# The tail of a Winograd convolution: inner rows transposed ahead of the last silu, the last 32 rows gathered by GpSimd

## The chip, the cores and the metric

The kernel runs on one core of a Trainium2 chip. The metric is the device time of one execution in microseconds (us). Three runs of the kernel before took 187.9, 187.98 and 188.08 us, so its median is 187.98. One execution more was profiled: it took 187.82 us, and the profile covers a span of 186.0 us of it.

## What is computed

A convolution of width 3 along the sequence, a batch norm with given mean and variance, and silu:

```python
xp = jnp.pad(x, ((0, 0), (1, 1), (0, 0)))          # x: 2 x 2048 x 1024, bf16
y = sum(jnp.einsum('bsc,cd->bsd', xp[:, k:k + S, :], w[k]) for k in range(3))
inv_std = 1.0 / jnp.sqrt(var + 1e-5)
y = (y - mean) * (g * inv_std) + b
return silu(y)                                     # 2 x 2048 x 1024, bf16
```

## The kernel before

**Tiling.** The convolution is done by Winograd's method: R = 6 rows of the output are made from 8 products (NJ = 8) instead of 18. The 2048 rows of one batch are NB = 342 blocks of 6 rows (the last block holds 2). TensorE first multiplies windows of x by a constant matrix (L322), and ScalarE or VectorE takes the result to `T_sb`: channels on the partitions, and for each of 8 positions one column per block. The weights of a tile of 128 output channels are turned into three pairs of sums and differences (`u0`, `u1`, `u2`), most of it by GpSimd (L188).

**Units.** A unit is one tile `dc` of 128 output channels and one batch `bi`, 16 in all, in the order of `dc` and then `bi`. A unit makes 8 products of 8 matmuls each (`product`, L368) into four of the eight PSUM banks, and neighbours alternate between banks 0 to 3 and 4 to 7. VectorE combines the products (L386), and ScalarE applies scale, bias and silu (`silu`, L391) and writes `yT`: 128 channels on the partitions, then 6 rows of a block, then 384 places for the blocks. Rows 1 to 4 of a block (inner) are ready when product 6 of the unit is combined. Row 0 and row 5 (outer) need one more product each, made with the raw weights `wch`.

**Stores.** For all but the last two units the DMA turns `yT` (`turn`, L554) into `o`, blocks on the partitions, and SP's queue stores `o` (`store`). For the last two units `put` (L515) turns the rows on TensorE against an identity (L525, one 128x128 transpose per row and group of 128 blocks), one copy brings them from PSUM to `o` (L526), and DMAs store them (L531). Blocks 336 to 341 (the last 32 rows of the batch) do not fit the DMA's shape and go out by `put_rest`: two small DMAs on GpSimd's queue, 30 rows (L542) and 2 rows (L546).

**The last unit** is cut in two halves: `h0`, the larger, holds blocks 128 to 341 in banks 4 to 7, and `h1` blocks 0 to 127 in banks 0 to 3. The order of the work is written out by hand (the program keeps the order of each engine as written). After the products 1 to 6 of h1 have been issued, the kernel before goes on so, L668 to L674:

- `h0.put(inner)`: 8 transposes into bank 5, one copy of 128x1024, two stores on SP's queue (128 and 80 blocks).
- `h1.silu_inner()`: two silus.
- `h1.both(...)`, L409: h1's product 0 into bank 0, then h0's outer rows (4 transposes into bank 6, a copy of 128x512, two stores on SP's queue), then product 7 into bank 3, then one silu that reads banks 0 and 3 as one strided operand and writes rows 0 and 5 of `yT`.
- `h1.put(inner)`: 4 transposes into bank 1, a copy of 128x512, a store on ScalarE's queue (ACTq).
- `h0.put_rest`: the two DMAs on GpSimd's queue.
- `h1.put(outer)`: 2 transposes into bank 2, a copy of 128x256, a store on ScalarE's queue.

Each DMA of SP's and ScalarE's queue counts on one of eight semaphores, in turn, and waits for the DMA eight before it. At the end of the program SP waits for these eight one after the other, in the order of their numbers, and then for the other engines.

`load_w` (L132) brings one of the three taps of the weights for a pair of tiles `dc` (L139), or for one of the two if `half` is given. The third pair after the first, tiles 6 and 7, is loaded behind unit 8 (L645).

Of the kernel before, what the change touches and what calls it, by code (L numbers as in the profile page):

```python
# [8 lines left out]
ACT = mybir.ActivationFunctionType  # L9
ALU = mybir.AluOpType  # L10
FP32 = mybir.dt.float32
BF16 = mybir.dt.bfloat16
# [3 lines left out]
P = 128  # L16
R = 6
# [9 lines left out]
def kernel(  # L27
# [10 lines left out]
    nc = tc.nc  # L38
    B, S, C = x.shape
    D = w.shape[2]  # L40
    CT, DC = C // P, D // P
    NB = -(-S // R)
# [22 lines left out]
    ps = pspool.tile([P, 8, 512], FP32, name="ps")  # L65
    T_sb = [tpool.tile([P, CT, NJ, NB], BF16, name=f"T_sb{bi}") for bi in range(B)]

    rows = consts.tile([4 * DC, P], BF16, name="rows")
# [63 lines left out]
    def load_w(pair, k, half=None):  # L132

        if (pair, "tile") not in raw:
            raw[pair, "tile"] = wpools[pair % 2].tile([P, 3, CT, 2, P], BF16, name=f"wch{pair % 2}")
        wch = raw[pair, "tile"]
        h0, h1 = (0, 2) if half is None else (half, half + 1)
        cols = slice((2 * pair + h0) * P, (2 * pair + h1) * P)
        nc.sync.dma_start(  # L139
            out=wch[:, k, :, h0:h1].rearrange("p c h d -> p c (h d)"), in_=w_all[:, k, :, cols]  # L140
        )
        clock["dma"] += 1400.0 * (h1 - h0)
        for h in range(2):
            raw[2 * pair + h] = wch[:, :, :, h]
# [3 lines left out]
    def idle(work):  # L148
        if work:
            work.pop(0)()  # L150
# [79 lines left out]
    def prepare_second(dc):  # L230


        w0, w2 = raw[dc][:, 0], raw[dc][:, 2]

        def times4(tap):
            t = spool.tile([P, CT, P], BF16, name="w1x2")
            nc.scalar.mul(t, tap, 4.0)
            busy("act", CT * P)
            return t

        def even(q, t, h):
            sums[dc, q] = epool.tile([P, CT, P], FP32, name=f"e{q}")
            nc.gpsimd.tensor_tensor(sums[dc, q], t, h, op=ALU.add)

        def first():
            even_part(dc, 0, nc.gpsimd)
            transform_w(dc, 0)

        def second():
            even(1, times4(w2), w0)  # L250

        def third():
            double_w(dc, nc.scalar)
            transform_w(dc, 1)

        def fourth():
            even(2, times4(w0), w2)
            transform_w(dc, 2)

        return first, second, third, fourth  # L260

    prm = consts.tile([P, 4, DC], BF16, name="prm")
    scale = consts.tile([P, DC], FP32, name="scale")
    beta = consts.tile([P, DC], FP32, name="beta")

    ident = consts.tile([P, P], BF16, name="ident")
# [77 lines left out]
    class Unit:  # L344
# [9 lines left out]
        def __init__(self, dc, bi, b0, lo=0, hi=NB):  # L354
            self.dc, self.bi, self.b0, self.lo, self.hi = dc, bi, b0, lo, hi
            self.bank = [ps[:, b0 + q, lo:hi] for q in range(4)]
            self.low, self.mid, self.high = (ps[:, b0 + q:b0 + q + 2, lo:hi] for q in range(3))
            self.yT = yts[bi]

        def product(self, q, j, add, between):  # L360
            dc = self.dc
            nsl = slice(self.lo, self.hi)
            for ct in range(CT):
                if j == 0 or j == NJ - 1:
                    lhsT = raw[dc][:, 0 if j == 0 else 2, ct]
                else:
                    lhsT = wts[dc, (j - 1) // 2][:, (j - 1) % 2, ct]
                nc.tensor.matmul(  # L368
                    self.bank[q], lhsT=lhsT, rhs=T_sb[self.bi][:, ct, j, nsl],
                    start=not add and ct == 0, stop=ct == CT - 1, skip_group_check=add,  # L370
                )
                clock["pe"] += (self.hi - self.lo) / 2.35
                between()
# [12 lines left out]
            nc.vector.scalar_tensor_tensor(out=out, in0=in0, scalar=scalar, in1=in1, op0=ALU.mult, op1=op1)  # L386
            busy("dve", (self.hi - self.lo) * (2 if len(out.shape) > 2 else 1))

        def silu(self, rows, src):
            dc = self.dc  # L390
            nc.scalar.activation(  # L391
                self.yT[:, rows, self.lo:self.hi], src, ACT.Silu, bias=beta[:, dc:dc + 1], scale=scale[:, dc:dc + 1]
            )

        def silu_inner(self):
            self.silu(slice(2, 4), self.y23)
# [7 lines left out]
        def last(self, between):  # L404

            self.product(3, NJ - 1, True, between)
            self.silu(R - 1, self.bank[3])

        def both(self, between, then):  # L409

            self.product(0, 0, True, between)
            then()
            self.product(3, NJ - 1, True, between)
            self.silu(slice(0, R, R - 1), ps[:, self.b0:self.b0 + 4:3, self.lo:self.hi])

        def run_first(self, between, left, following):

# [97 lines left out]
        def put(self, o, rows, bank, evac, queues, blocks=None):  # L515

            i0, i1 = min(rows), max(rows)
            every = slice(i0, i1 + 1, 1 if i1 == i0 else (i1 - i0) // (len(rows) - 1))
            blocks = blocks or range(self.lo // P, -(-self.hi // P))
            n = min(self.hi - self.lo, P)  # L520
            v = ps[:, bank].bitcast(BF16)[0:n, 0:len(rows) * len(blocks) * P]
            v = v.rearrange("p (i k d) -> p i k d", i=len(rows), k=len(blocks))
            for a, i in enumerate(rows):
                for q, k in enumerate(blocks):
                    nc.tensor.transpose(v[:, a, q], self.yT[:, i, k * P:k * P + n], ident)  # L525
            evac(o[0:n, every, blocks[0]:blocks[-1] + 1], v)  # L526
            outs = out[self.bi, :, self.dc * P:(self.dc + 1) * P]
            full = S // R
            for q, k in zip(queues, blocks):
                hi = min((k + 1) * P, full // 16 * 16)  # L530
                q.dma_start(  # L531
                    out=outs[k * P * R:hi * R].rearrange("(p i) d -> p i d", i=R)[:, every],
                    in_=o[0:hi - k * P, every, k],
                )

        def put_rest(self, o, queue):

            full = S // R
            lo = full // 16 * 16
            k, p0 = lo // P, lo % P  # L540
            rows = out[self.bi, :, self.dc * P:(self.dc + 1) * P]
            queue.dma_start(  # L542
                out=rows[lo * R:full * R].rearrange("(p i) d -> p i d", i=R), in_=o[p0:p0 + full - lo, :, k]
            )
            k, p0 = full // P, full % P
            queue.dma_start(  # L546
                out=rows[full * R:S].rearrange("(p i) d -> p i d", p=1), in_=o[p0:p0 + 1, 0:S % R, k]
            )
# [51 lines left out]
    class Between:  # L600


        n = done = 0
# [20 lines left out]
    between = Between()  # L624
# [3 lines left out]
    for i, (dc, bi) in enumerate(seq[:-1]):  # L628
        unit = Unit(dc, bi, i % 2 * 4)
        if i == 0:  # L630
            unit.run_first(between, left[0], prepare_second(1))
        else:
            unit.run(
                between,
                prev.rest_first(between) if i == 1 else
                prev.rest(between, *((4, 5) if i >= len(seq) - 3 else (5, 4) if i == 2 else (5, 6)))
                + ([(1, lambda: idle(act_work)), (1, lambda: idle(dve_work))] if i == 3 else []),
                2 if i == 2 else dc + 2 if bi == 1 and 0 < dc < DC - 2 else None,
                i == 2,
            )  # L640
        if i == 0:
            xwin_scope.close()
            olast = ctx.enter_context(tc.tile_pool(name="olast", bufs=3))
            wpools[1] = ctx.enter_context(tc.tile_pool(name="wpool1", bufs=1))
        if i in (0, 4, 8):  # L645
            for k in range(3):
                load_w(i // 4 + 1, k)
        if i == len(seq) - 2:
            prev.turn(olast, ((1, R), (0, 1)))
        elif prev:  # L650
            prev.turn()
        if before:
            before.store(late if i == len(seq) - 2 else ())
        before, prev = prev, unit
    before.store(late)
    dc, bi = seq[-1]
    sp, ac = nc.sync, nc.scalar
    inner, outer = tuple(range(1, R - 1)), (0, R - 1)
    to_v, to_s = nc.vector.tensor_copy, nc.scalar.copy
    o = olast.tile([P, R, NK, P], BF16, name="o")  # L660
    h0 = Unit(dc, bi, 4, P, NB)
    h0.run(between, prev.rest(between, 5, 5) + [(5, lambda: prev.put(o, inner, 1, to_v, (sp, sp), (0, 1)))])
    h1 = Unit(dc, bi, 0, 0, P)
# [2 lines left out]
        (3, lambda: prev.put(o, inner, 1, to_s, (sp,), (2,))), (3, lambda: prev.put_rest(o, nc.gpsimd)),  # L666
    ] + h0.rest(between, 5, 6))
    o2 = olast.tile([P, R, NK, P], BF16, name="o")  # L668
    h0.put(o2, inner, 5, to_v, (sp, sp))
    h1.silu_inner()  # L670
    h1.both(between, lambda: h0.put(o2, outer, 6, to_v, (sp, sp)))
    h1.put(o2, inner, 1, to_v, (ac,))
    h0.put_rest(o2, nc.gpsimd)
    h1.put(o2, outer, 2, to_v, (ac,))  # L674

_INS = ['x', 'w', 'mean', 'var', 'g', 'b']
# [25 lines left out]
```

## Time and profile before

| what | us |
|---|---|
| median of three runs | 187.98 |
| the profiled execution | 187.82 |
| its span in the profile | 186.0 |
| TensorE busy (PE) | 177.8, 96% of the span |
| VectorE (DVE) / ScalarE (ACT) / GpSimd (POOL) busy | 152.3 / 113.1 / 147.6 |
| start of the last matmul of a product | 180.73 |
| last store issued, on ScalarE's queue | 183.05 |

Times within the profile count from the span's start. PE is TensorE's matmuls and PEld its loads of weights, which overlap them. SPq, ACTq and POOLq are the sequencers that issue DMAs; "SPq ... DMA" is the issue and not the transfer. A row of the timeline gives start, length, engine, line of the kernel, operation, output and input, and in brackets how long the engine had been idle and what released it. A group of several instructions (x4) runs from the first one's start to the last one's end. A row of stages gives the busy time of each engine between two times, the granted clock of TensorE, the mean busy share of the 16 DMA engines, and what they moved.

### The profile page before, as it was taken

How to read it: one execution, taken by the hardware profiler on the slowest of the kernel's cores; microseconds unless marked ns; L12 is line 12 of the kernel's file. 1: busy time of each engine (PE TensorE's matmuls, PEld its weight loads, DVE VectorE, ACT ScalarE, POOL GpSimd, SP SyncE). 2: the span in 40 equal slices, each digit the busy share in tenths (PEclk: the TensorE clock that was granted, in tenths of full speed). 3: DMA queues.
4: the chain of work that ended last, by engine and by line, in shares of the span. 5: the costliest groups of instructions: out<-in, count | busy, mean ns of one | idle time of the engine just before them, and what ended most of it. 6: DMA issues, size and time to landing. Idle time of an engine off the chain costs nothing.

```text
span 186.0 us, 3724 instructions
## 1 busy us (share of the span) xinstructions
PE 177.8 (96%) x1402; PEld 125.5 (67%) x1402; DVE 152.3 (82%) x212; ACT 113.1 (61%) x183; POOL 147.6 (79%) x90
## 2 busy tenths in 40 slices
PE   6889999999999999999999999999999999999991
PEld 2658688866666666666666666666666666669990
DVE  5368777997769999999988998879988996769781
ACT  3599888896647565456545654565456556363790
POOL 7198899999997979999999999999999972020122
PEclk9999999999999999999999999999999999999997
DMA  5999999066426855798849657986474967779734
GB/s 168 329 345 329 385 388 234 5 191 154 83 44 59 186 112 128 195 200 188 161 113 206 116 127 196 194 193 126 117 143 107 210 100 164 141 160 172 166 75 113
DMA packets 87022, 31.72 MB, mean 171 GB/s; under 512 B 73606, under 2 KB 82842, under 8 KB 87004
## 3 DMA queue, kind: packets, MB, share of 16 engines
q1 hardware_dynamic: 85820, 31.24, 72.5%
q10 hardware_dynamic: 800, 0.20, 0.4%
q8 instruction: 11, 0.18, 0.4%
q0 software_dynamic: 384, 0.04, 0.3%
q14 instruction: 7, 0.06, 0.1%
HBM read 14.82 MB, written 8.39 MB: 125 GB/s over the span
## 4 chain that ended last, share of the span: by engine, by line
PE 85%; SPq 4%; DVE 4%; DMA 3%; ACT 1%; issue 1%; DVEq 0%
PE ps L368 79%; PE ps L322 5%; SPq L123 3%; DVE T_sb L335 3%; DMA xw<-in_x_dram 3%; ACT T_sb L333 1%; PE ps L525 1%; SPq L139 0%; DVE sd L386 0%; ACT yT L391 0%; DVEq L697 0%; DVE o L526 0%; DVEq L335 0%
## 5 line engine op out<-in xcount | busy, mean ns | idle before, releaser
L368 PE MATMUL ps<-T_sb,u 128*128 128x342 bf16 (+2 forms) x816 | 120.1, 299 | 0.1
L368 PEld LDWEIGHTS <-u 128*128 128x128 bf16 x816 | 76.8, 97 | 33.4 <-issue 0.2
L188 POOL TENSOR_TENSOR u<-e,w1x 128x1024 bf16<-128x1024 f32 x32 | 69.4, 2191 | 3.9 <-DVE e L169 2.4
L368 PE MATMUL ps<-T_sb,wch 128*128 128x342 bf16 (+2 forms) x272 | 42.6, 299 | 0.4 <-ACT T_sb L333 0.4
L391 ACT ACTIVATE yT<-ps,beta,scale 128x342 bf16<-128x342 f32 (+4 forms) x50 | 34.1, 712 | 13.3 <-PE ps L368 13.3
L188 POOL TENSOR_TENSOR u<-e,wch 128x1024 bf16<-128x1024 f32 x16 | 38.5, 2426 | 1.6 <-DMA wch<-in_w_dram 1.0
L386 DVE SCALAR_TENSOR_TENSOR t<-ps,sd 128x684 f32<-128x684 f32 (+2 forms) x51 | 39.0, 821 | 0.6
L368 PEld LDWEIGHTS <-wch 128*128 128x128 bf16 x272 | 25.7, 97 | 12.0 <-issue 0.7
L379 ACT COPY pc<-ps 128x342 f32<-128x342 f32 (+2 forms) x35 | 15.0, 428 | 28.7 <-PE ps L368 28.4
L333 ACT CAST T_sb<-ps 128x1008 bf16<-128x1008 f32 (+2 forms) x31 | 25.8, 870 | 7.4 <-PE ps L322 7.1
L335 DVE CAST T_sb<-ps 128x1008 bf16<-128x1008 f32 (+2 forms) x19 | 20.7, 1115 | 10.4 <-PE ps L322 10.4
L386 DVE SCALAR_TENSOR_TENSOR ps<-ps,t 128x684 f32<-128x684 f32 (+2 forms) x34 | 28.3, 831 | 0.6
L322 PE MATMUL ps<-rm,xw 128*128 128x168 bf16 (+2 forms) x272 | 25.1, 235 | 1.5 <-DMA xw<-in_x_dram 0.6
L169 DVE SCALAR_TENSOR_TENSOR e<-wch 128x1024 f32<-128x1024 bf16 x12 | 25.9, 2158 | 0.0
L322 PEld LDWEIGHTS <-xw 128*128 128x128 bf16 (+2 forms) x272 | 20.5, 99 | 7.3 <-issue 3.5
L386 DVE SCALAR_TENSOR_TENSOR ps<-ps,pc 128x342 f32<-128x342 f32 (+2 forms) x34 | 16.9, 496 | 9.2 <-PE ps L368 7.8
L167 POOL TENSOR_TENSOR e<-wch 128x1024 f32<-128x1024 bf16 x7 | 16.9, 2409 | 0.5 <-DMA wch<-in_w_dram 0.5
L391 ACT ACTIVATE yT<-t,beta,scale 128x684 bf16<-128x684 f32 (+2 forms) x17 | 15.7, 924 | 0.0
L386 DVE SCALAR_TENSOR_TENSOR t<-ps,t 128x684 f32<-128x684 f32 (+2 forms) x17 | 13.9, 817 | 0.0
L567 POOL DMA_DIRECT2D out_dram<-o x2 | 1.3, 657 | 15.8 <-DMA o<-yT 15.8
L386 DVE SCALAR_TENSOR_TENSOR sd<-pc,ps 128x342 f32<-128x342 f32 (+2 forms) x17 | 8.2, 484 | 6.4 <-ACT sd L379 6.3
L379 ACT COPY sd<-ps 128x342 f32<-128x342 f32 (+2 forms) x17 | 7.3, 429 | 9.6 <-PE ps L368 9.0
(55 smaller groups left out, 61.3 us busy)
## 6 DMA issues: line engine op xcount, KB each, us to landing
xw<-in_x_dram SPq DMA_DIRECT2D x32, 256.0 KB
out_dram<-o SPq DMA_DIRECT2D x28, 192.0 KB
wch<-in_w_dram SPq DMA_DIRECT2D x9, 512.0 KB
out_dram<-o SPq DMA_DIRECT2D x14, 120.0 KB
wch<-in_w_dram SPq DMA_DIRECT2D x6, 256.0 KB
out_dram<-o SPq DMA_DIRECT2D x3, 128.0 KB
o<-yT SPq DMA_TRANSPOSE x15
out_dram<-o SPq DMA_DIRECT2D x12, 7.5 KB
```

What stands on the lines that cost most here:

```text
L123: nc.sync.dma_start(out=xw[0:hi - lo, :], in_=x[bi, lo:hi, :])
L167: eng.tensor_tensor(e, w0, w2, op=ALU.add)
L169: eng.scalar_tensor_tensor(out=e, in0=f, scalar=4.0, in1=h, op0=ALU.mult, op1=ALU.add)
L188: nc.gpsimd.tensor_tensor(wts[dc, q][:, i], sums[dc, q], o, op=(ALU.add, ALU.subtract)[i])
L322: nc.tensor.matmul(v[:, q, c], lhsT=xw[0:rows, (c0 + c) * P:(c0 + c + 1) * P], rhs=mat[0:rows, :, 0:n], start=True, stop=True,)
L333: nc.scalar.copy(dst, src)
L335: nc.vector.tensor_copy(dst, src)
L368: nc.tensor.matmul(self.bank[q], lhsT=lhsT, rhs=T_sb[self.bi][:, ct, j, nsl], start=not add and ct == 0, stop=ct == CT - 1, skip_group_che ...
L379: nc.scalar.copy(dst, self.bank[q])
L386: nc.vector.scalar_tensor_tensor(out=out, in0=in0, scalar=scalar, in1=in1, op0=ALU.mult, op1=op1)
L391: nc.scalar.activation(self.yT[:, rows, self.lo:self.hi], src, ACT.Silu, bias=beta[:, dc:dc + 1], scale=scale[:, dc:dc + 1])
L525: nc.tensor.transpose(v[:, a, q], self.yT[:, i, k * P:k * P + n], ident)
```

## The change

- `h1`'s last silu writes a tile of its own (`outer`, 128x256) instead of two rows of `yT`, and `put` reads from it for h1's outer rows.
- `h1`'s inner rows are turned in bank 4 instead of 1, and the program places their transposes before that silu (`last`, called inside `both`). Their store is issued later, by `send`, which is cut out of `put`.
- h0's last six blocks go another way (`put_end`): GpSimd copies their 36 columns of `yT` (6 blocks x 6 rows) into `y`, in the order of the output's rows; one transpose on TensorE brings them to bank 5, VectorE copies 32 rows to `end`, and one DMA on ScalarE's queue stores these. It is the first of three on that queue. `put_rest` of h0 is gone.
- h0's inner rows are turned as two groups, blocks 128 to 255 into bank 5 and 256 to 341 into bank 6, with a copy and a store each; h0's outer rows move to bank 7.
- The load of tap 0 for tiles 6 and 7 is cut into two halves.

```diff
@@ Unit
+            self.outer = None
-        def silu(self, rows, src):
+        def silu(self, rows, src, dst=None):
             dc = self.dc
-            nc.scalar.activation(
-                self.yT[:, rows, self.lo:self.hi], src, ACT.Silu, bias=beta[:, dc:dc + 1], scale=scale[:, dc:dc + 1]
-            )
+            if dst is None:
+                dst = self.yT[:, rows, self.lo:self.hi]
+            nc.scalar.activation(dst, src, ACT.Silu, bias=beta[:, dc:dc + 1], scale=scale[:, dc:dc + 1])
-        def both(self, between, then):
+        def both(self, between, then, outer, last):
             self.product(0, 0, True, between)
             then()
             self.product(3, NJ - 1, True, between)
-            self.silu(slice(0, R, R - 1), ps[:, self.b0:self.b0 + 4:3, self.lo:self.hi])
+            last()
+            self.outer = outer
+            self.silu(None, ps[:, self.b0:self.b0 + 4:3, self.lo:self.hi], outer)
@@ put
-                    nc.tensor.transpose(v[:, a, q], self.yT[:, i, k * P:k * P + n], ident)
+                    src = self.yT[:, i, k * P:k * P + n] if self.outer is None else self.outer[:, a]
+                    nc.tensor.transpose(v[:, a, q], src, ident)
             evac(o[0:n, every, blocks[0]:blocks[-1] + 1], v)
+            if queues:
+                self.send(o, every, blocks, queues)
+            return every, blocks
+
+        def send(self, o, every, blocks, queues):
             outs = out[self.bi, :, self.dc * P:(self.dc + 1) * P]
...
+        def put_end(self, o, bank, evac):
+            lo = S // R // 16 * 16
+            n, rows = (NB - lo) * R, S - lo * R
+            y = olast.tile([P, n], BF16, name="y")
+            nc.gpsimd.tensor_copy(
+                y.rearrange("d (t i) -> d t i", i=R), self.yT[:, :, lo:NB].rearrange("d i t -> d t i")
+            )
+            v = ps[0:n, bank].bitcast(BF16)[:, 0:P]
+            nc.tensor.transpose(v, y, ident)
+            evac(o[0:rows], v[0:rows])
@@ the loop over the units
-            for k in range(3):
-                load_w(i // 4 + 1, k)
+            for k, half in ((0, None), (1, None), (2, None)) if i < 8 else ((0, 0), (0, 1), (1, None), (2, None)):
+                load_w(i // 4 + 1, k, half)
@@ the end
-    h0.put(o2, inner, 5, to_v, (sp, sp))
+    h0.put(o2, inner, 5, to_v, (sp,), (1,))
+    h0.put(o2, inner, 6, to_v, (sp,), (2,))
     h1.silu_inner()
-    h1.both(between, lambda: h0.put(o2, outer, 6, to_v, (sp, sp)))
-    h1.put(o2, inner, 1, to_v, (ac,))
-    h0.put_rest(o2, nc.gpsimd)
+    done = []
+    end = olast.tile([S - S // R // 16 * 16 * R, P], BF16, name="end")
+
+    def last():
+        h0.put_end(end, 5, to_v)
+        done.extend(h1.put(o2, inner, 4, to_v, ()))
+
+    h1.both(
+        between, lambda: h0.put(o2, outer, 7, to_v, (sp, sp)), olast.tile([P, 2, P], BF16, name="outer"), last
+    )
+    ac.dma_start(out=out[bi, S // R // 16 * 16 * R:S, dc * P:(dc + 1) * P], in_=end)
+    h1.send(o2, *done, (ac,))
     h1.put(o2, outer, 2, to_v, (ac,))
```

## The prediction

> **What bounds the kernel now.** I read the page's busy times and chain of waits first, then the chain and the timeline of the last 6 us, the stages of the same stretch, and the groups of GpSimd.
>
> ```profile
> PE 177.8 (96%) x1402; PEld 125.5 (67%) x1402; DVE 152.3 (82%) x212; ACT 113.1 (61%) x183; POOL 147.6 (79%) x90
> ...
> PE 85%; SPq 4%; DVE 4%; DMA 3%; ACT 1%; issue 1%; DVEq 0%
> ```
>
> TensorE carries 85% of the chain that ended last. Nothing in the change shortens TensorE's stream, so a gain can only come behind its last product. The timeline there:
>
> ```profile
> 180.39 1.16 ACT L391 ACTIVATE yT<-ps,beta,scale 128x256 bf16<-128x256 f32 x2
> 180.70 0.41 DVE L526 COPY o<-ps 128x512 bf16<-128x512 bf16 x1
> 180.73 0.22 PE L368 MATMUL ps<-T_sb,wch 128*128 128x128 bf16 x1
> 180.81 2.01 SPq L531 DMA_DIRECT2D out_dram<-o  x4
> 180.99 0.10 PEld L525 LDWEIGHTS <-yT 128*128 128x128 bf16 x1 [0.22 <-ACT yT L391]
> 181.40 0.60 POOL L542 DMA_DIRECT2D out_dram<-o  x1 [2.60 <-DVE o L526]
> 181.60 0.49 PE L525 MATMUL ps<-ident,yT 128*128 128x128 bf16 x6 [0.65 <-ACT yT L391]
> ...
> 182.00 0.52 POOL L546 DMA_DIRECT2D out_dram<-o  x1
> 182.08 0.62 DVE L526 COPY o<-ps 128x512 bf16<-128x512 bf16 x2 [0.97 <-ACT yT L391]
> 182.54 0.98 ACTq L531 DMA_DIRECT2D out_dram<-o  x2
> ```
>
> The second of the two silus at 180.39 is the last one (180.99, 0.56 long). h1's inner rows were ready at 180.94, and their first weights are loaded at 180.99, but all six transposes start at 181.60, when the last silu is over. Then they run one after the other into one copy, one store, and the next: copies at 182.08 (0.42) and 182.42 (0.28), issues at 182.54 and 183.05, 0.51 apart. The second issue is the last work: its packets end at 184.58 (the packet rows), 1.53 behind the issue, and its semaphore is full at 184.92. SP passes that wait at 184.94, makes two waits more, 0.06 apart each, and the span ends at 185.97. The stages show what the DMA engines do meanwhile:
>
> ```profile
> 181.60:182.60 1.00, 0.49 (x6) 0.32 (x5) 0.52 (x2) 0.00 (x0) 0.92 (x2) 1.00 0.71 169
> 182.60:183.40 0.80, 0.00 (x0) 0.00 (x0) 0.10 (x1) 0.00 (x0) 0.00 (x0) 1.00 0.75 154
> 183.40:184.60 1.20, 0.00 (x0) 0.00 (x0) 0.00 (x0) 0.00 (x0) 0.00 (x0) 0.69 0.82 194
> 184.60:186.00 1.40, 0.00 (x0) 0.00 (x0) 0.00 (x0) 0.00 (x0) 0.00 (x0) 0.50 0.00 0
> ```
>
> The last two columns are the share of the DMA engines and GB/s: 0.71 to 0.82, busy but not full, from h0's first packet at 181.72 on. So the tail has two limits close together: the last issue, and the DMA engines.
>
> **Part by part.** *Inner rows ahead of the silu.* In the built program the four inner transposes wait only for the second inner silu (180.94). They load weights at 180.99 as now, and now follow through: starts at about 181.09 to 181.26 at the 0.055 spacing of the rows. Today 0.31 lies between the start of the fourth one (181.77) and the copy behind it (182.08), so the copy runs 181.57 to 181.99. The outer transposes wait for the silu (181.55): weights at 181.60, matmuls at 181.69 and 181.75, copy at 182.06 to 182.34. Today the outer copy ends at 182.70.
>
> *The three stores on ScalarE's queue.* `end` is issued when VectorE has copied it (181.4, below), or behind the silu at 181.56; both are early enough. The inner store goes out at 182.03 (copy 181.99 plus the 0.03 to 0.04 seen now) and the outer one 0.51 later, **182.54 instead of 183.05: 0.51 gained**. If the first issue were to start only at 181.6, its 0.51 leads to 182.11 and 182.62: 0.43. With the same 1.53 to the last packet it ends at 184.07.
>
> *The DMA engines.* The first h0 store now waits for a copy of 128x512 instead of 128x1024 (0.42 for 0.68), so it goes out at 180.55 instead of 180.81, and SP's other three issues follow at the same spacing: 0.26 earlier. Two copies of 0.42 take 0.16 more than one of 0.68; h0's outer copy ends at 181.19 instead of 181.11 and is still ahead of its issue (181.6; now 181.86). Packets now are 256 bytes, 0.018 long, on 16 engines: 875 per us. By the packet rows SP's queue has about 205 left 1.56 behind its first one, thus 205 + 32 of `end` + 768 of h1 from 183.02 on: 1005 in 1.15 us, plus the 0.08 by which the same count misses the end now, gives 184.25. The DMA limit is later than the issue limit by 0.18, both are estimates, and the two small DMAs of GpSimd, whose 64 packets ran among these, are gone: I take 184.15, **0.43 gained**.
>
> *The last waits.* In the built program the last store counts on the sixth of the eight semaphores now, and on the eighth in the changed one; that is what the halved weight load shifts. SP then goes from its wait straight to the end: **0.12 gained**. GpSimd's drain, which now lasts 2.81 us to 184.64 behind its last DMA, has nothing to wait for.
>
> *The gather.* h0's last silu ends at 179.95; GpSimd is free from 178.81. These are its small operations:
>
> ```profile
> L291 POOL TENSOR_TENSOR sc<-sc,mhalf 128x8 f32<-128x8 f32 x1 | 1.7, 1676 | 0.1
> ...
> L292 POOL TENSOR_TENSOR sc<-prm,sc 128x8 f32<-128x8 bf16 x1 | 0.2, 201 | 0.1
> ...
> L290 POOL TENSOR_SCALAR sc<-prm 128x8 f32<-128x8 bf16 x1 | 0.2, 194 | 4.2 <-ACT prm L283 4.2
> ```
>
> A copy of 128x36 is not among them. Ends: 0.19 (L290) and 1.68 (L291, a power, and the first operation of two operands); I take 0.25, as a plain operation of few columns costs 0.20 and 1024 columns 1.05 (L211), so 0.85 ns a column. `y` is there at 180.25. TensorE wants it at 180.79, and loses nothing until 180.94, where it waits for the inner silu anyway: slack 0.7. A gather of 1.68 is at 181.68 and delays everything behind it (third rival). The transpose of `y` is one matmul more in that gap; VectorE copies 32x128 from 181.1 in about 0.21 (128x256 takes 0.28, 512 columns 0.42) to 181.4, ahead of the inner copy at 181.57. Cost nothing; without the gap 0.06 on TensorE.
>
> *The halved load.* 512-byte packets take 0.027, 256-byte ones 0.018, so 2048 of the latter instead of 1024 of the former take 2.30 instead of 1.73 on 16 engines: the weights of tiles 6 and 7 land 0.6 later, and one SP issue is added (0.4 to 0.6). GpSimd already waits 0.47 for that load at 120.91, so its sums for tiles 6 and 7 move by 0.6 to 1. The cover: those of tile 6 are done at 137.57, and TensorE begins with tile 6 at 139.47 and comes to the last pair 4.6 later; those of tile 7 end at 154.56, and it begins at 156.89. The transposing DMA of unit 7 behind the loads lands at 122.56; the silu that waits for it runs at 127.25. Cost nothing; a delay over 2.3 would show on TensorE one for one.
>
> **Sum.** 0.43 + 0.12 = 0.55 off the profiled execution's 187.82: 187.27. The median of the runs is 0.16 above that execution; on its scale 187.98 - 0.55 = **187.43**, a gain of 0.3%. A measurement of this kernel tells about 0.2% (0.38 us) from no change, so the line lies at 187.60.
>
> **Rivals.** *The DMA engines are the end.* The stores' 504 KB keep their pace however early ScalarE issues, so all that helps is h0's first store, 0.26 earlier, with or without the 0.12 of the last waits: 187.60 to 187.72. For it: shares of 0.71 to 0.82 from 181.6 on. Against it: from 183.0 to 183.4 the rate falls to about half of the best, between SP's last packets and ScalarE's first, a hole that earlier issues fill. Chance 0.24. The Trainium skill, "DMA: Bandwidth & Descriptors", section "Issuing engines are not separate DMA queues", states that DMAs of any issuing engine end on the same 16 engines and only sequencer time is saved. The two queues sharing the engines at 183.4 to 183.8 agree with it, and by that rule alone this rival's time would come.
>
> *The false wait stays.* If the inner transposes wait for the last silu after all, copies stay at 182.08, three issues follow, and the first of them (`end`) is out before: 187.86 from the last waits alone, or 187.60 with h0's earlier store. The built program has no such wait: chance 0.04.
>
> *GpSimd is late: slower.* TensorE's queue holds all six last transposes behind `y`. From a gather of about 0.95 on, each us costs one. At 1.68 `y` is ready at 181.68; four and two transposes follow from 181.7 to 182.05, the three copies end at 182.9 and the last issue is at about 183.3, 0.25 later than now: less 0.12 this is 188.1. From about 1.95 the change is slower by over 0.2%, 188.4 and more. For it: no copy on GpSimd stands in the trace, and L291 may be a first call's cost as well as a power's. Against it: the first memset, ramp, select and scalar operation at the span's start took 0.10 to 0.29. Chance 0.06. The Trainium skill, "GPSIMD Engine Reference", section "2.1 Instruction dispatch", states that the first call to a freshly loaded routine pays about 6 us; no first call in this trace shows that, and with it the time would be some 5 us longer.
>
> **How the numbers follow.** Forecast, 187.2 to 187.60: 0.62. A larger gain, down to 187.05, if the issue limit alone holds (184.07) and the 64 packets and the drain that went away count too: 0.04. Rivals: 0.24, 0.04, 0.06. Faster by over 0.2% is 0.62 + 0.04 and a part of the first rival, 0.02: 0.68; the same 0.26; slower 0.06. The range from 187.10 to 187.86 leaves out a very large gain and the late gather.
>
> **What would show it.** Right: in the changed profile the inner transposes start at about 181.1, before the last silu ends; the inner copy is near 181.57; three issues on ACTq, the last near 182.5; last packet near 184.1; SP has no wait behind the last store's. The gather lasts about 0.25 and ends before 180.8. The first SP issue of h0 is near 180.55. Wrong: TensorE idle behind 180.95 waiting for POOL; the last packet 1.7 or more behind the last issue (the DMA engines); TensorE waiting for `u` at 139 or 157.

## The result and the profile after

Six executions of the changed kernel have a median of 187.33 us (186.99 to 187.48), six of the kernel before, run with them, 188.05 (187.9 to 188.7): a ratio of 0.996, with a 95% interval of 0.9944 to 0.9976. The profiled execution took 187.41 us with a span of 185.5 (before 187.82 and 186.0). The forecast was 187.43.

The two lines of the changed kernel's page that answer to those of before, busy times and chain of waits:

```profile
PE 178.0 (96%) x1403; PEld 125.9 (68%) x1403; DVE 153.0 (82%) x214; ACT 112.9 (61%) x183; POOL 146.8 (79%) x89
...
PE 85%; DMA 5%; DVE 4%; ACT 2%; SPq 1%; issue 0%; DVEq 0%; ACTq 0%
```

TensorE does not get shorter, it has one matmul more. What is new lies behind its last product. The timeline of the changed kernel from there (start, length, engine, line, operation):

```profile
179.98 0.24 POOL L551 COPY y<-yT 128x36 bf16<-128x36 bf16 x1 [1.22 <-ACT yT L394]
...
180.51 2.02 SPq L541 DMA_DIRECT2D out_dram<-o  x4
180.84 0.09 PEld L555 LDWEIGHTS <-y 128*36 128x36 bf16 x1
...
180.95 0.56 ACT L394 ACTIVATE outer<-ps,beta,scale 128x256 bf16<-128x256 f32 x1
181.00 0.23 PEld L530 LDWEIGHTS <-yT 128*128 128x128 bf16 x4
181.01 0.40 PE L530 MATMUL ps<-ident,yT 128*128 128x128 bf16 x4
181.11 0.21 DVE L556 COPY end<-ps 32x128 bf16<-32x128 bf16 x1
181.36 0.39 ACTq L704 DMA_DIRECT2D out_dram<-end  x1
181.51 0.73 DVE L531 COPY o<-ps 128x512 bf16<-128x512 bf16 x2 [0.19 <-ACT outer L394]
181.57 0.11 PEld L530 LDWEIGHTS <-outer 128*128 128x128 bf16 x2 [0.34 <-ACT outer L394]
...
181.97 1.02 ACTq L541 DMA_DIRECT2D out_dram<-o  x2
```

The four inner transposes run at 181.01, beside the last silu, where before all six stood behind it at 181.60. The three issues on ScalarE's queue are at 181.36, 181.97 and 182.49 (the last two are one row). The last one is 0.56 earlier than before. But the last packet ends at 184.26 by the packet rows, only 0.32 earlier than before: 1.77 behind the last issue, for 1.53. The stages, in the windows of the prediction (last two columns: share of the DMA engines, GB/s):

```profile
181.60:182.60 1.00, 0.26 (x2) 0.08 (x2) 0.63 (x2) 0.00 (x0) 0.00 (x0) 1.00 0.86 196
182.60:183.40 0.80, 0.00 (x0) 0.00 (x0) 0.00 (x0) 0.00 (x0) 0.00 (x0) 1.00 0.80 180
183.40:184.60 1.20, 0.00 (x0) 0.00 (x0) 0.00 (x0) 0.00 (x0) 0.00 (x0) 0.94 0.60 128
184.60:186.00 1.40, 0.00 (x0) 0.00 (x0) 0.00 (x0) 0.00 (x0) 0.00 (x0) 0.50 0.00 0
```

The first two shares were 0.71 and 0.75. What was moved earlier filled the engines, and the third stage is emptier for it.

The last store lands at 184.92 before and at 184.59 after. From there to its first drain SP makes two waits fewer (line, engine, operation, count: min/median/max in ns, first and last start). Before, the wait for the last store and two more:

```profile
L697 SPq EVENT_SEMAPHORE  x3: 28/28/28, 184.9 to 185.1; - x3
```

After, the wait for the last store alone:

```profile
L729 SPq EVENT_SEMAPHORE  x1: 28/28/28, 184.6 to 184.6; - x1
```

From the last landing to SP's drain it is 0.20 before and 0.10 after. So the span is 0.43 shorter: 0.03 because the last product starts earlier (180.70 for 180.73), 0.29 by the last packet, 0.01 from that packet to its landing, and 0.10 behind the landing.

### The profile page after: what moved, and what is told of

It is laid out like the page before. It is cut to its first block, busy times and chain, and to the rows that moved or that the text cites. A ratio compares the mean times of both kernels' runs of the same rounds, so it can differ in the third digit from the quotient of the medians.

```text
span 185.5 us, 3732 instructions
## 1 busy us (share of the span) xinstructions
PE 178.0 (96%) x1403; PEld 125.9 (68%) x1403; DVE 153.0 (82%) x214; ACT 112.9 (61%) x183; POOL 146.8 (79%) x89
## 4 chain that ended last, share of the span: by engine, by line
PE 85%; DMA 5%; DVE 4%; ACT 2%; SPq 1%; issue 0%; DVEq 0%; ACTq 0%
PE ps L369 79%; DMA xw<-in_x_dram 5%; PE ps L322 5%; DVE T_sb L335 3%; SPq L123 1%; ACT T_sb L333 1%; PE ps L530 1%; DVE sd L387 0%; DVE o L531 0%; ACT outer L394 0%; DVEq L335 0%; ACTq L333 0%
## 5 line engine op out<-in xcount | busy, mean ns | idle before, releaser
L394 ACT ACTIVATE yT<-ps,beta,scale 128x342 bf16<-128x342 f32 (+4 forms) x49 | 33.5, 713 | 13.3 <-PE ps L369 13.3
```

The lines of the kernel that those rows point to most:

```text
L394: nc.scalar.activation(dst, src, ACT.Silu, bias=beta[:, dc:dc + 1], scale=scale[:, dc:dc + 1])
```

## The experiments

**Theories.** *Issue theory:* the end is the last issue and a fixed time behind it. *Engine theory:* the end is set by the DMA engines, by when their stream of packets starts and how long it is. *Drain theory:* GpSimd's drain ends a fixed time behind the landing of its own last DMA, and where it does so late, it ends the program.

**The measure.** Over the 14 profiles the first product starts anywhere from 19.39 to 20.17 us, in a part that no kernel here changes, and this alone moves the time of one execution by up to 0.78. So I read each profile from the start of the last product's last matmul to the end of the span, and call that the **tail**. All issues and packets in the table count from the same point. Where a run's VectorE order delays the last product itself, the text says so.

| kernel | tail | h1's inner store issued | last issue | last packet ends | median, us (ratio to before, 95%) |
|---|---|---|---|---|---|
| before | 5.24 | 1.81 | 2.32 | 3.85 | 188.05 |
| after | 4.85 | 1.27 | 1.79 | 3.56 | 187.33 (0.996, 0.9944 to 0.9976) |
| after_again | 4.84 | 1.27 | 1.78 | 3.56 | 187.56 (0.9986, 0.9974 to 0.9998) |
| late_inner | 5.05 | 1.81 | 2.30 | 3.77 | 187.72 (0.9985, 0.9967 to 1.0004) |
| one_copy | 5.02 | 1.27 | 1.77 | 3.69 | 187.69 (0.9974, 0.9957 to 0.9991) |
| no_outer_store | 4.63 | 1.27 | 1.77 | 3.23 | 187.14 (0.9944, 0.9923 to 0.9965) |
| pool_rest | 5.29 | 1.22 | 1.77 | 3.63 | 188.02 (0.999, 0.9972 to 1.0008) |
| pool_rest_again | 5.28 | 1.22 | 1.77 | 3.60 | 187.86 (0.9996, 0.998 to 1.0013) |
| gather_only | 5.13 | 1.81 | 2.30 | 3.79 | 187.82 (0.9997, 0.9982 to 1.0012) |
| whole_load | 4.91 | 1.27 | 1.79 | 3.59 | 187.47 (0.9974, 0.996 to 0.9987) |
| spread | 4.76 | 1.27 | 1.71 | 3.34 | 187.46 (0.9978, 0.9966 to 0.9991) |
| spread_end | 4.96 | 1.48 | 1.57 | 3.50 | 187.68 (0.9993, 0.9973 to 1.0013) |
| early_copy | 4.51 | 1.27 | 1.76 | 3.23 | 187.53 (0.9978, 0.9959 to 0.9996) |
| spread_early | 4.63 | 1.33 | 1.58 | 3.30 | 187.45 (0.9975, 0.9958 to 0.9991) |

The median of before was 188.18 on the chip of the runs late_inner to pool_rest (without its repeat), 187.95 on that of after_again, gather_only, whole_load and spread, and 187.81 on that of the rest.

**after_again.** The changed kernel once more.

> The changed kernel once more, nothing edited, on the chip and day of the kernels beside it. Between the profiles so far the first product starts anywhere from 19.4 to 20.0, so spans differ by 0.6 for reasons ahead of the tail; the tail (from the start of the last product's last matmul to the span's end) was 5.24 before and 4.85 in the changed kernel. If that 4.85 is no accident, this run's tail is 4.75 to 4.95, and the median 0.4 to 0.7 under the kernel before's.

The tail repeats to 0.01. The median repeats less well: it is 0.72 under the kernel before's in the first comparison and 0.39 in this one. By the ratios of the table the gain is 0.75 (0.45 to 1.05) in the first and 0.26 (0.04 to 0.49) in this one. The tail's 0.39 to 0.40 lies between these two.

**late_inner.** h1's inner transposes back behind the last silu, in bank 1:

```diff
     def last():
         h0.put_end(end, 5, to_v)
-        done.extend(h1.put(o2, inner, 4, to_v, ()))
...
+    rows_0_5, h1.outer = h1.outer, None
+    done.extend(h1.put(o2, inner, 1, to_v, ()))
+    h1.outer = rows_0_5
     ac.dma_start(out=out[bi, S // R // 16 * 16 * R:S, dc * P:(dc + 1) * P], in_=end)
```

> Undoes one part of the change alone: h1's inner rows go into bank 1 behind the last silu again, so their four transposes wait for it; the rest is as changed. In the changed kernel's profile the last product's last matmul starts at 180.70, the last store on ScalarE's queue is issued at 182.49, the last packet ends at 184.26 and the span at 185.5. Issue theory (the end is the last issue plus a fixed time): the inner copy runs from 182.05 and the last issue moves to about 183.02, 0.53 later, so the last packet ends 0.4 to 0.5 later and the run takes 187.8. Engine theory (the end is set by when the DMA engines get their first packet and how many there are; earlier issues only fill holes): the packets of SP's queue keep their times, the hole before h1's packets opens again, last packet at about 184.4, 0.15 later, and the run takes 187.5.

Its transposes and issues in the timeline:

```profile
181.83 0.38 PE L530 MATMUL ps<-ident,yT 128*128 128x128 bf16 x4 [0.49 <-ACT outer L394]
...
182.76 0.95 ACTq L541 DMA_DIRECT2D out_dram<-o  x2
```

The last issue is 0.51 later than in after, the last packet 0.21 and the tail 0.20. By the issue theory the packet had to come 0.4 to 0.5 later. Stages of late_inner, from 2.0 to 3.6 behind the last product:

```profile
182.96:183.36 0.40, 0.00 (x0) 0.00 (x0) 0.00 (x0) 0.00 (x0) 0.00 (x0) 1.00 0.45 105
183.36:183.76 0.40, 0.00 (x0) 0.00 (x0) 0.00 (x0) 0.00 (x0) 0.00 (x0) 1.00 0.45 97
183.76:184.16 0.40, 0.00 (x0) 0.00 (x0) 0.00 (x0) 0.00 (x0) 0.00 (x0) 1.00 0.89 218
184.16:184.56 0.40, 0.00 (x0) 0.00 (x0) 0.00 (x0) 0.00 (x0) 0.00 (x0) 1.00 0.81 213
```

And of after, the same distances:

```profile
182.70:183.10 0.40, 0.00 (x0) 0.00 (x0) 0.00 (x0) 0.00 (x0) 0.00 (x0) 1.00 0.73 156
183.10:183.50 0.40, 0.00 (x0) 0.00 (x0) 0.00 (x0) 0.00 (x0) 0.00 (x0) 1.00 0.82 186
183.50:183.90 0.40, 0.00 (x0) 0.00 (x0) 0.00 (x0) 0.00 (x0) 0.00 (x0) 1.00 0.99 203
183.90:184.30 0.40, 0.00 (x0) 0.00 (x0) 0.00 (x0) 0.00 (x0) 0.00 (x0) 1.00 0.61 142
```

Earlier issues close a hole of 0.8 us in which the engines were at less than half load, and so 0.51 of them is worth 0.21. What still earlier issues would win this run does not show; spread, below, moves some of them and gains on the last packet again.

**one_copy.** h0's inner rows by one copy of 128x1024 again, as before:

```diff
-    h0.put(o2, inner, 5, to_v, (sp,), (1,))
-    h0.put(o2, inner, 6, to_v, (sp,), (2,))
+    h0.put(o2, inner, 5, to_v, (sp, sp))
...
-        h0.put_end(end, 5, to_v)
+        h0.put_end(end, 6, to_v)
```

> Undoes one part alone: h0's inner rows go into one bank and out by one copy of 128x1024, as before; both stores wait for it. The first h0 store should go out at 180.77 instead of 180.51, and the last store on ScalarE's queue stay at 182.49. Its last store counts on the seventh of the eight semaphores instead of the eighth, which is one wait of 0.06 more under either theory. Issue theory: last packet unchanged at 184.26, 187.4. Engine theory: the whole stream of packets starts 0.26 later and ends 0.2 to 0.26 later, at about 184.5, 187.65.

SP's first store is issued at 0.07 instead of -0.19, SP's other three 0.21 to 0.27 later, and the last packet ends 0.13 later, with ScalarE's issues where they were; the other 0.04 of its 0.17 lies behind the last landing, where SP has one wait more. So the start of SP's stream counts too, for half of what it is moved.

**no_outer_store.** h0's two outer stores are not issued:

```diff
-        between, lambda: h0.put(o2, outer, 7, to_v, (sp, sp)), ...
+        between, lambda: h0.put(o2, outer, 7, to_v, ()), ...
```

> Leaves out work: h0's two outer stores (128x2 and 80x2 rows of 256 bytes, 104 of 512 KB in the tail) are not made, so those rows of the output stay unwritten. Nothing else moves; the last store is issued at 182.49. Issue theory: last packet 184.26 as now. Engine theory: 416 packets less, at 875 a us up to 0.48; the stores of h1 are then bound by their own issue, so the last packet ends at 183.8 to 183.95, 0.3 to 0.45 earlier, and the run takes 187.0.

The last packet comes 0.33 earlier, with the same last issue on ScalarE's queue. That is the plainest word against the issue theory. Yet 416 packets fewer should be worth 0.48 at the prediction's 875 per us, were the engines full throughout. Its stages show why they are not (2.0 to 2.8 behind the last product):

```profile
183.14:183.54 0.40, 0.00 (x0) 0.00 (x0) 0.00 (x0) 0.00 (x0) 0.00 (x0) 1.00 0.36 86
183.54:183.94 0.40, 0.00 (x0) 0.00 (x0) 0.00 (x0) 0.00 (x0) 0.00 (x0) 1.00 0.90 218
```

A hole opened ahead of h1's inner rows.

**pool_rest and pool_rest_again.** The gather taken out, `put_rest` on GpSimd's queue back, all else as in after; run twice, on two chips:

```diff
-        h0.put_end(end, 5, to_v)
...
-    ac.dma_start(out=out[bi, S // R // 16 * 16 * R:S, dc * P:(dc + 1) * P], in_=end)
+    h0.put_rest(o2, nc.gpsimd)
```

> Undoes the gather alone: h0's last 32 rows go out by the two small DMAs on GpSimd's queue again, and no copy, transpose and store of their own are there; inner rows are still ahead of the silu. One store fewer on ScalarE's queue, whose last issue should stay at 182.49 since the copies set it; one semaphore wait of 0.06 more at the end. If the gather itself is worth something, the two DMAs' 64 packets among the others cost up to 0.07, or GpSimd's drain (2.1 behind its last issue before, so now about 184.4) holds the end, which it should not by 0.3. Both theories: 0.06 to 0.13 later than the changed kernel, 187.4 to 187.45. If the gather were what carries the gain, 187.7 or more.

> The same kernel as pool_rest, to see whether what ended it repeats: GpSimd's last DMA landed there 3.95 behind the last product's start, 0.545 later its drain ended, and that was the program's last work (tail 5.29, 0.15 behind SP's own end). Drain theory: GpSimd's drain ends 0.5 to 0.6 behind the landing of its own last DMA again, and the tail is the later of that and of SP's end: 5.2 to 5.3 if that DMA lands at 3.9 again, 5.1 if it lands earlier. Issue and engine theory: the drain has nothing to wait for, tail as after's, 4.85, and 0.06 for the lane order at most.

Both times the whole gain is gone (5.29 and 5.28, before 5.24), though the last packet is as early as in after, within 0.07. The rows of the end-of-program line for the second run (count, then min/median/max in ns, first and last start):

```profile
L728 POOLq DRAIN  x3: 51/102/3327, 182.0 to 185.8; - x3
L728 SPq DRAIN  x3: 7/7/13, 185.1 to 185.6; - x3
```

GpSimd's drain of 3327 ns starts at 181.97 and ends at 185.30, 0.15 behind SP's second drain, and the closing signals of all engines follow it. Its last DMA landed at 184.75, 0.55 earlier. In after, SP's drains stand here:

```profile
L729 SPq DRAIN  x3: 7/7/13, 184.7 to 185.0; - x3
```

In before, GpSimd's drain is not the last thing:

```profile
L697 POOLq DRAIN  x3: 51/102/2811, 181.8 to 185.7; - x3
```

It ends at 184.64 there, also 0.55 behind its DMA's landing at 184.09, and SP's first drain comes at 185.13. So the drain theory holds for what ends the program without the gather: GpSimd's last DMA, issued 0.06 later than before, lands 0.6 later (3.94 for 3.36 behind the last product), and its drain takes the end. That it lands late because the other packets now crowd it is argued, not shown. But the drain is not the whole of the 0.43 that is lost against after. SP's second drain itself ends 4.34 behind the last product, in after 4.07, so 0.27 would be lost without GpSimd's drain, which adds 0.16. Of the 0.27, 0.04 is the later last packet, 0.04 is SP's longer way from the last landing to its drain (it has one wait more there), and 0.19 is a landing 0.52 behind the last packet instead of 0.33. The cause of that late landing is open (see spread_end).

**gather_only.** The kernel before, with the gather and nothing else of the change:

```diff
-    h1.both(between, lambda: h0.put(o2, outer, 6, to_v, (sp, sp)))
+    end = olast.tile([S - S // R // 16 * 16 * R, P], BF16, name="end")
+    h1.both(between, lambda: h0.put(o2, outer, 6, to_v, (sp, sp)), lambda: h0.put_end(end, 7, to_v))
+    ac.dma_start(out=out[bi, S // R // 16 * 16 * R:S, dc * P:(dc + 1) * P], in_=end)
     h1.put(o2, inner, 1, to_v, (ac,))
-    h0.put_rest(o2, nc.gpsimd)
```

> The kernel before with the gather alone: h0's last 32 rows by a copy on GpSimd, a transpose and a store on ScalarE's queue; the inner rows still wait for the last silu, h0's inner rows go out by one copy, weights load whole. Drain theory (GpSimd's drain ends 0.54 to 0.55 behind the landing of its own last DMA, in the profile before at 184.64 and without effect, in the run that put only these DMAs back at 185.55 and past SP's last wait at 185.41; so in a good part of the executions before, it is GpSimd that ends the program): the median falls by 0.2 to 0.4 against the kernel before, though this profile's tail is only 5.1 to 5.2. Engine theory alone: 64 small packets less, tail 5.15 to 5.2, median 0.05 to 0.1 lower, nothing that can be measured.

The tail gains 0.11. The median gains 0.06 by the ratio, with an interval from a loss of 0.23 to a gain of 0.34. So the drain theory's larger claim, that in many executions GpSimd ends the kernel before, finds no support here, though the interval does not shut it out; in before's profile that drain ends 0.55 ahead of SP's second one. The two halves do not add up: the gather alone gives 0.11, all else alone gives -0.04, both give 0.39.

**whole_load.** The load of tap 0 not halved:

```diff
-            for k, half in ((0, None), (1, None), (2, None)) if i < 8 else ((0, 0), (0, 1), (1, None), (2, None)):
+            for k, half in ((0, None), (1, None), (2, None)):
```

> The changed kernel with tap 0 of tiles 6 and 7 loaded whole again, as before. Its last store counts on the seventh of eight semaphores, so SP makes one wait of 0.06 more: tail 4.9. The weights land at 120.7 as they did before and in the changed kernel, where halving them cost nothing, so nothing else moves. If the halving is worth more than that wait, tail 5.0 or more.

The tail is 0.07 longer than after's, 0.05 of it between the last landing and the end: the halved load is worth one wait of SP. The median cannot tell it.

**spread.** The late stores dealt out anew: h0's last outer store goes to ScalarE's queue, h1's outer one to SP's, and the last 32 rows go last:

```diff
-        between, lambda: h0.put(o2, outer, 7, to_v, (sp, sp)), ...
+        between, lambda: h0.put(o2, outer, 7, to_v, (sp,)), ...
...
+    h0.send(o2, slice(0, R, R - 1), (2,), (ac,))
+    h1.send(o2, *done, (ac,))
     ac.dma_start(out=out[bi, S // R // 16 * 16 * R:S, dc * P:(dc + 1) * P], in_=end)
-    h1.send(o2, *done, (ac,))
-    h1.put(o2, outer, 2, to_v, (ac,))
+    h1.put(o2, outer, 2, to_v, (sp,))
```

> The changed kernel with its last stores dealt out differently: h0's second outer store on ScalarE's queue as soon as its copy is done (181.18 in the changed profile's times instead of 182.04 on SP's), then h1's inner rows (181.97 as now), then the 32 gathered rows (182.48 instead of 181.36); h1's outer rows last on SP's queue (182.28 instead of 182.49). Issue theory: the last large store goes out 0.2 earlier, tail 4.6 to 4.7. Engine theory: the stream starts as now at 0.74 behind the last product but has its holes filled (0.57 of the engines busy at 182.8, and 0.79 at 183.2); 2080 packets at 875 a us would end at 183.8 instead of 184.26, so tail 4.45 to 4.7. If neither, a second queue with two stores at once slows both and the tail stays at 4.85.

The last packet is 0.22 earlier, the tail only 0.09, less than either theory gave: the last landing came 0.48 behind the last packet, in after 0.33.

**spread_end.** As spread, with the last 32 rows ahead of h1's inner rows on ScalarE's queue:

```diff
     h0.send(o2, slice(0, R, R - 1), (2,), (ac,))
+    ac.dma_start(out=out[bi, S // R // 16 * 16 * R:S, dc * P:(dc + 1) * P], in_=end)
     h1.send(o2, *done, (ac,))
-    ac.dma_start(out=out[bi, S // R // 16 * 16 * R:S, dc * P:(dc + 1) * P], in_=end)
```

> Spread with one order changed: on ScalarE's queue the last 32 rows go out ahead of h1's inner rows, and not behind. So the inner store is issued at about 1.5 for 1.27, the small one at 1.0 for 1.71. Both theories have the last issue on SP's queue at 1.58. Issue theory: as spread, last packet 3.34, tail 4.76, less the 0.15 if the small store's landing set the end there. Engine theory: 256 packets (of h1's inner rows) go out 0.2 later while the engines still have h0's to carry, so the last packet is within 0.05 of 3.34; the last landing is 0.33 behind it and not 0.485: tail 4.60 to 4.70. If the tail stays at 4.76, the late landing in spread does not come from that store's place.

A miss of every theory. h1's inner store is issued 0.21 later than in spread and the small store 0.75 earlier, all else is the same, and the last packet is 0.16 later, though the last issue is not later. Its issues in the timeline:

```profile
181.86 0.39 ACTq L541 DMA_DIRECT2D out_dram<-o  x1
...
182.34 0.42 ACTq L705 DMA_DIRECT2D out_dram<-end  x1
182.86 0.45 ACTq L541 DMA_DIRECT2D out_dram<-o  x1
```

Nor did the late landing go away (0.46 behind the last packet), so it does not come from the small store's place. What makes it 0.32 to 0.35 in most profiles and 0.46 to 0.52 in four (these two and both of pool_rest) stays open.

**early_copy and spread_early.** h0's first inner copy put ahead of h1's last combine on VectorE, in after and in a spread kernel (ScalarE's queue: h0's outer rows 256 to 341, the last 32 rows, h1's inner rows; h1's outer rows on SP's):

```diff
-        def run(self, between, also=(), prepare=None, later=False):
+        def run(self, between, also=(), prepare=None, later=False, hold=False):
...
+            if hold:
+                behind(6)
...
-            behind(6)
+            if not hold:
+                behind(6)
...
+    o2 = olast.tile([P, R, NK, P], BF16, name="o")
...
-    ] + h0.rest(between, 5, 6))
-    o2 = olast.tile([P, R, NK, P], BF16, name="o")
-    h0.put(o2, inner, 5, to_v, (sp,), (1,))
+    ] + h0.rest(between, 5, 6) + [(6, lambda: h0.put(o2, inner, 5, to_v, (sp,), (1,)))], hold=True)
```

> After, with one order on VectorE changed: h0's copy of blocks 128 to 255 (0.42) stands ahead of h1's last combine and no longer behind it, so SP's first store of h0 can go out about 0.33 earlier (-0.52 of the start of the last product's last matmul, for -0.19 in after), and the combine, h1's inner silus and with them product 7 of h1 are late by up to 0.2. Tail: from that matmul to the span's end, 4.85 in after. Issue theory (the end is the last issue and a fixed time): the last issue does not come earlier, so the tail stays 4.85 or grows by what the inner copy is late, up to 0.2. Engine theory (the end is set by when the stream of packets starts and how many there are; one_copy, with a start 0.26 later, lost 0.13): 0.10 to 0.17 off the last packet, tail 4.70 to 4.78. In both, the time of TensorE's last products is up to 0.2 longer, so the median by the engine theory is within 0.1 of after.

> The early copy of the run before, and the stores spread so that each queue has one issue less in a row: ScalarE's queue carries h0's outer store of blocks 256 to 341, then the last 32 rows, then h1's inner rows; SP's carries h0's two inner stores, h0's outer one of 128 to 255 and at the end h1's outer rows. Issue theory: the last issue is at 1.58, as in spread, 0.21 earlier than in after: tail 4.64 and not lower. Engine theory: start 0.33 earlier and the late packets issued earlier by 0.2 both fill holes; last packet 3.2 (3.56 in after, 3.34 in spread), tail 4.5 to 4.6. In spread the last landing came 0.485 behind the last packet; if the late small store on ScalarE's queue made that, it goes back to 0.33 here, since that store is no longer the queue's last.

The last product is late by 0.23 in both, as VectorE's combine is; with that their tails compare as 4.74 and 4.86 to after's 4.85. In early_copy the last packet is 0.33 earlier behind that product, twice what the engine theory gave, with ScalarE's issues unmoved. Its stage from 2.0 to 2.4:

```profile
184.00:184.40 0.40, 0.00 (x0) 0.00 (x0) 0.00 (x0) 0.00 (x0) 0.00 (x0) 1.00 0.49 113
```

The hole is back. Of the 0.33, 0.23 is paid for in the last product. spread_early's tail of 4.63 is in number what the issue theory gave (4.64), though late_inner and no_outer_store speak against that theory; its last packet came at 3.30, where the engine theory gave 3.2. By the tail, with the last product counted, spread is 0.09 and early_copy 0.11 better than after; by the median no run that does all the work is better by more than its interval.

**What remains of the theories.** Neither the last issue nor the start alone sets the end. An account that fits was formed after these runs and is not tested on a further kernel: take each store's packets as ready 1.05 after its issue, and let the engines send 810 packets per us in the order of issue. The stores are 512 and 320 packets (h0 inner), 256 and 160 (h0 outer), 32 (the last rows), 512 and 256 (h1); no_outer_store is without the 416. Both numbers are fitted to ten of the profiles, and give the last packet of each within 0.09 (root mean square 0.05). For three of the other four they give it too early, by 0.12 in whole_load, 0.21 in pool_rest and 0.18 in its repeat (GpSimd's 64 packets, which are not in the sum, would make up at most 0.08 of that). By this account the last packet depends on the issue that ends the last hole. In before this is h1's inner store: 1.81 + 1.05 + 768 / 810 = 3.81 (measured 3.85). In after it is the same store, but h0's last outer store (160), issued 0.08 behind it, now shares the stretch: 1.27 + 1.05 + 928 / 810 = 3.47 (3.56). In late_inner 3.81 (3.77), in no_outer_store and early_copy 3.27 (3.23 both), in spread_end 1.48 + 1.05 + 0.95 = 3.48 (3.50). In one_copy and spread no hole is left, and all 2048 packets count from SP's first issue: 0.07 + 1.05 + 2.53 = 3.65 (3.69), and 3.39 (3.34).

## Why the prediction was right, and where it was not

- **The inner rows ahead of the silu: right.** Transposes at 181.01 to 181.19 (forecast 181.09 to 181.26), copies at 181.51 and 181.95 (181.57, 182.06). Undoing it alone costs 0.20 of the tail.
- **The three stores on ScalarE's queue: right**, at 181.36, 181.97, 182.49 (181.4, 182.03, 182.54).
- **The DMA engines: the mis-sized term.** Of the forecast's 0.43, 0.32 came, 0.03 of them from TensorE's earlier end. The count of packets had given 184.25, and the last one ended at 184.26; I took 184.15, between this and the issue limit. A mean of two limits has no ground; the later of them came true. That the count met 184.26 is luck in part: at 183.02 it had 1005 packets left, by the packet rows there were 897 of 256 bytes, and they went out at some 725 per us and not at 875. The sign that the prediction named for the engines, a last packet 1.7 or more behind the last issue, is there with 1.77. Why the 0.53 that h1's inner store gained (1.81 to 1.27) gave 0.29 is told by the fit alone, made afterwards: 160 packets more lie behind it, 0.20.
- **h0's first store: right in time** (180.51, forecast 180.55). It is worth 0.13 by one_copy.
- **The last waits: nearly right**, 0.10 for 0.12. whole_load shows one of the two as the halved load's.
- **The gather: its cost right, its worth missed.** The copy's row, by shape (total us and mean ns, then idle time ahead):

```profile
L551 POOL COPY y<-yT 128x36 bf16<-128x36 bf16 x1 | 0.2, 238 | 1.2 <-ACT yT L394 1.2
```

  It took 0.238 for the estimate of 0.25, and `y` was ready at 180.22, forecast 180.25. L291's 1.68 was no guide. The Trainium skill's "GPSIMD Engine Reference", section "2.1 Instruction dispatch", has about 6 us for the first call to a freshly loaded routine; this first copy shows nothing of it. But that the drain "has nothing to wait for" was put down as a remark with no price. Without the gather 0.43 is lost: pool_rest has all else and gains nothing. Of this, 0.16 is that drain, which then has a late DMA to wait for, 0.19 is a late landing with no cause found, and the rest is a later packet and SP's longer way behind the landing. The question to ask was where GpSimd's DMAs land beside stores that now go out earlier, and it was not asked.
- **The halved load: no cost, but not for the reason given.** The forecast had the weights land 0.6 later, hidden. Tap 0 itself was later: its second half was full at 117.40, the whole tap before at 115.74. But GpSimd waits for the third tap too, which is loaded last and whole, and that one was full at 120.73, before at 120.76; GpSimd went on at 120.89, before at 120.91. Most of the load's packets were later (all but 100 of them had ended at 119.34, before at 118.41), the last one was not (120.17 and 120.16). What holds that one back no run here took apart.
- **The sum and the rivals.** The profiled execution lost 0.41, forecast 0.55. That lies between the forecast and the engine rival (0.26 to 0.38), so 0.24 was too little for that rival: half of its mechanism was at work. "By that rule alone this rival's time would come", the prediction said of the Trainium skill's sentence on the shared engines ("DMA: Bandwidth & Descriptors", section "Issuing engines are not separate DMA queues"). no_outer_store agrees that the engines are shared, 0.33 for another queue's stores. But with the inner rows late they stood half empty ahead of the last stores (0.45 in late_inner), and there earlier issues paid. The median's 187.33 meets 187.43 closer than the reasons deserve, and in part by luck: its gain was 0.72 in the first comparison and 0.39 in the repeat, for a forecast of 0.55, and the tail has 0.39. The false wait did not stay, and GpSimd was not late.

## What to carry to other kernels

When several stores end a kernel, write down for each its issue time and its packets, and work out the stream: look for the last hole, for the issue that closes it, and for what is left to send from there; in these runs the last packet moved with these. Then look at what lies behind it, the landing, the last waits and the drains, which made 0.10 of the gain here and most of the loss without the gather. Ask of each part that "costs nothing" also what would take over if it were not there: the parts here gained 0.11 and -0.04 alone and 0.39 together. For gains of this size, measure from a fixed point near the end of the trace, as the start alone varies by more (0.78 here).

## What the runs showed of the hardware

- GpSimd's drain at the end of the program ended 0.55 behind the landing of its own last DMA in three profiles with late DMAs (before, pool_rest, pool_rest_again). In the last two it ended the program, about 0.16 later than SP alone would have.
- The last landing came 0.32 to 0.35 behind the last packet in most profiles and 0.46 to 0.52 in four, with no cause found.
- The time from the start to the first product varied from 19.39 to 20.17 between executions; from there to the last product it was 161.08 to 161.21 in eleven of the fourteen profiles. It was 161.34 in spread_early and 162.13 in early_copy, where the last product is late by 0.23, and 161.90 in spread, where nothing ahead of the tail was edited: one execution can lose 0.8 there too.
